# A new order for the opening of a fused attention, two-layer and soft-mixture kernel

## The chip, the cores and the metric

The kernel runs on one core of one Trainium2 chip. The number that counts is the device time of one execution in microseconds (us). A core has five engines with a queue of instructions each: PE (TensorE, the matrix engine), DVE (VectorE), ACT (ScalarE), POOL (GpSimd) and SP (SyncE, which here only issues DMAs). Each engine runs its own queue strictly in order and waits on semaphores for the others, so an instruction that waits holds up all that stands behind it on its engine.

## The reference

Three parts follow one another; all data is float32.

```python
scores = scale * np.matmul(q, k.transpose(0, 1, 3, 2))      # 4 batches, 8 heads, 576 tokens, 64 wide
scores = np.where(masks[None], scores, -1e9)                # heads 0-3: the last 32 tokens; 4-7: every 32nd token
attn = softmax(scores)
x = np.matmul(attn, v)                                      # regrouped to 2304 tokens x 512
...
h = x @ w_in                                                # 512 -> 2048
r = np.maximum(h, 0.0)
x = (r * r) @ w_out                                         # 2048 -> 512
...
logits = x @ phi                                            # 32 slots
d = softmax over tokens;  slot_input = d.T @ x
slot_out[e] = np.maximum(slot_input[e] @ w1[e], 0.0) @ w2[e]    # 8 experts, 4 slots each
out = softmax over slots @ slot_out
```

## The kernel before, in words

The 2304 tokens are handled in six blocks of 384. A block has twelve **steps** of PE work, step s = 12b + 3c + j for block b, quarter c of the 2048 hidden columns and 128 tokens j. One step is twelve matmuls of 128x128 by 128x512 (`gemm1`, line 462): four parts kc of the contraction, three matmuls each, because activations and weights are split into a rounded high part and the rest (low part). Its result goes through relu (`square`), a square (`sq`, on ACT or POOL) and a transposition on DVE (`bt_`, into the tile `gt`), and after three steps `logits` multiplies `gt` by a small matrix `pt`, which is phi folded into w_out beforehand (`matrix`: product `pp` on PE, copy to `lsb` on ACT, product `pr` on PE, transposition into `pt` on DVE). After four such `logits` the block's softmax and slot sums follow (`Dispatch`).

Attention comes in **units**: a batch and a pair of heads. Unit n of the opening is 0 to 3 for batch 0 (pairs 0 to 3) and 4 to 7 for batch 1 (pairs 2, 0, 3, 1; those of pairs 0 and 1 are first halves, part A). Pairs 0 and 1 are local, pairs 2 and 3 strided. A unit loads q, two halves of k, and v; it makes masked scores (`qa`), exponentials, a normalised copy, transposes that (for units 0 to 3 through the PSUM tile `turned`, for the others by DVE), multiplies by v (`oa`, `ob`), and writes high and low parts into the tile `xr` that the steps read. Step 0 needs the units 0 to 3.

The weights come raw, 512 KB a load (`raw0` to `raw15` for w_in, `raw16` to `raw31` for the transposed w_out), as 64-bit words that must be taken apart: `convert(m)` handles raw 2m and 2m+1 by reading the upper words (ACT, line 427), a shift (DVE, line 430) and two combinations (DVE, line 434). For w_in two casts to the high part (ACT) and two subtractions (DVE or POOL, line 443) follow.

All this is woven together in the **opening**, whose order is written out by hand: the string `HEAD` is a list of tokens, and the loop over `HEAD.split()` issues each token's instructions at that place of every queue that they use. q, v and l are loads (unit's q and k, unit's v, raw weight), w is a number of dummy matmuls, A is the next piece of a unit, C the next piece of a conversion, P the next piece of a `pt` matrix, G one kc of a step, R its relu, X its square, T its transposition, L a `logits`; f loads phi, H and Z give memory over. A letter A, D or P at the end picks the engine. Behind the opening a loop over steps puts everything else at fixed places between the steps.

Loads that are issued by SP go out in order, at most eight outstanding: each waits until the one eight places ahead has landed, and, where it overwrites a buffer, until the last reader has finished. Units 0 and 3 to 7 share one buffer for q and k, and the units from 4 on one buffer for v.

Of the kernel before, what the change touches and what calls it, by code (L numbers as in the profile page):

```python
# [17 lines left out]
NB_ATT, H, S, D = 4, 8, 576, 64  # L18
# [15 lines left out]
RAW_AT = [0, 1, 2, 20, 21, 22, 23, 0, 1, 2, 23, 0, 1, 2, 0, 1]  # L34
NY = 4
HEAD = """
l1 l0 q2 l4 q1 l8 l9 w10 A0 A2 A0 q3 v0 l3 l2 C0 A0 C0 A0 w2 A0 C0 C0 A2 C0 A0 A2 C0 w1 A1 A0 C0 C0P A0 C2 A2
A0D A1 C0P A2 A2 A0 A1 C4 A1 C4 A3 A2 A0A A1 C4 A0A A0D A2P C4 A0A A3 q4 v1 l11 l7 v2 l22 l5 l6 l16 f l18 v3
l14 A0A C4 A0A A1 A0D A0D C4 A3 w3 A0 v4 A1 C4 C1 C4D C4P A2 A0 A1 A0 A0 A3 A1P C1 A0 G0 A2A A2A C1 A2A A4 A2A
A2A C1 A2A A4 q5 l17 l10 l15 l21 A2A A2A C1 C1 A1 A4 A3 C1 C1D A4 A3 C1P A1A A1D A4 A3 A1A A2 A1A A4 A3P A1D  # L40
A2 A1D A2 A1D A2 A4 A2 A1A A2 A4P C2 A2 w4 A3 A2 C3 A2 C2 C3 A1 A3D C8 A3D C2 G0 A3A A3A A1 C2 A1 A1 A3A A3A
A1 A3A w1 G0 A3A C3 C2 A3 C3 C2 A4 C2D C2P A3 H A3 C3 A3 A3 A3 C3 A3 A3 C3 C3P A3 A4D w3 A5 A4D A4A G0 C3P C8
A5 A4A G1 A4D R0 C8 C5 G1 A5 X0P C5 C8 l23 l13 G1 C7 C8 A5 A4A G1 C5 C7 G2 A5 T0 A4A G2 R1 A5 C5 G2 X1A C5 C5
G2 A5 C5 G3 C5P A4D T1 R2 Z A4 v5 l19 l12 q6 l24 C7 G3 A4 C5P C7 G3 A4 A4 C7 G3 A4 A5P A4 C9 G4 A4 X2P C7 A5
G4 A5 C7 A5 A5 G4 C7P R3 A5 A4 G4 A5 C9 X3P A5 G5 A5 R4 A4 G5 C7D C6 X4P A5 T2 C6 G5 C11 C9 G5 C11 C6 A6 A5 C9
l25 R5 G6 C11 A6 q7 v6 l20 X5A A5 G6 C11 G6 C11 l27 G6 A6 G7 C9 R6 C6 A6 C12 P0 C6 C12 G7 A6 C12 P0 G7 A6 C6
P0 C12 C6 C6P A7 A6 X6A G7 P0 A6P A7 C12 l29 l26 l28 R7 G8 C6P A6 L0 A6 X7P C10 A6 C10 G8 A6 G8 C10 G8 T5 G9
C10 R8 G9 C10 C13 G9 A7 C13 T4 P1 X8A C13 C14 A7 T3 G9 P1 C13 A7 G10 C14 C13 A6 v7 l30 R9 A7 G10 C14 X9A G10
A6 A7 C14 l31 A6 A7P G10 A6 C14 A6 G11 R10 A6 G11 A6 X10A A6 G11 A6 A7 P1 A7 C15 A7 G11 A7 P1 P2 C15 A7 A7 L1
R11 A7 C15 P2 A7 X11P C15 P2 C15 A7 P2 A7 A7 T7 P3 T6 P3 T8 P3 L2 P3 T9 T11 T10 L3  # L50
"""
ATT_END = 48
EPS = 1e-9
# [21 lines left out]
def body(tc, qd, kd, vl, vs, win, wout, woutt, phi, w1, w2, cst, out):  # L75
    nc = tc.nc
    PE, ACT, DVE, POOL, SP = nc.tensor, nc.scalar, nc.vector, nc.gpsimd, nc.sync

    with ExitStack() as base, ExitStack() as order:
        def pool(stack, name, bufs=1, side="left", space=None, **kw):  # L80
            if space is not None:
                return stack.enter_context(tc.tile_pool(name=name, bufs=bufs, space=space, **kw))
            return stack.enter_context(tc.tile_pool(name=name, bufs=bufs, side=side, **kw))
# [16 lines left out]
        def ps(tag, name):  # L100
            if tag in ("t", "lg", "mo"):
                return late[0].tile([128, 512], F32, tag=tag, name=name, bufs={"t": 2, "lg": 1, "mo": 1}[tag])
            return pp.tile([128, 512], F32, tag=tag, name=name, bufs=2)

        c = cp.tile([128, C_END], F32, name="c")
# [25 lines left out]
        def slot(n, shape, dt, name):  # L131
# [11 lines left out]
        bufs = [  # L143
            b0,
            Buf(hp.tile([128, S + 16], F32, name="q1"), hp.tile([128, KW], F32, name="k1"),
                hp.tile([128, 8, 128], F32, name="v1"), hp.tile([128, 10, 64], F32, name="sl1"), None, None),
            Buf(hp.tile([128, S + 16], F32, name="q2"), hp.tile([128, KW], F32, name="k2"),
                hp.tile([128, 8, 128], F32, name="v2"), None, b0.ss, b0.sw),
            b0.but(v=hp.tile([128, 8, 128], F32, name="v3"), ss=hp.tile([128, 16, 18], F32, name="s3"),
                   sw=hp.tile([128, 16, 32], F32, name="sw3")),  # L150
        ]

        def load_qk(b, p, u, part="AB", queue=None):
            n = S if "B" in part else T // 2
            SP.dma_start(u.q[:, :n], qd[b, p, :, :n])
            (queue or SP).dma_start(u.k[0:64, 32:32 + n], kd[b, p, 0:64, :n])
            SP.dma_start(u.k[64:128, 32 + S:32 + S + n], kd[b, p, 64:128, :n])

        def load_v(b, p, u, part="AB"):
# [293 lines left out]
        def where(s):  # L453
            return s // 12, s % 12 // 3, s % 3

        def gemm1(s, kcs=range(4)):
            b, ch, j = where(s)
            if s not in hs:
                hs[s] = [ps("h", f"h{s}"), 0]
            for kc in kcs:  # L460
                for x, a in ((0, 0), (0, 1), (1, 0)):
                    PE.matmul(hs[s][0], xr[b % 3][:, x, kc, 128 * j:128 * j + 128], w_in[ch, kc][:, a],  # L462
                              start=hs[s][1] == 0, stop=hs[s][1] == 11)
                    hs[s][1] += 1
# [150 lines left out]
        def load_e_pair(a, b):  # L615
            load_e(lambda name: [a, b])

        def load_e_slot(n):
            load_e(lambda name: slot(n, [128, 2, 512], F32, name))

        def load_e_ring(n):
            t = ringp.tile([128, 6, 512], F32, tag=f"ring{n}", bufs=1, name=f"ring{n}_{e_next[0]}")
            for y in range(3):
                load_e(lambda name: t[:, 2 * y:2 * y + 2])

        def load_e_raw(n):
            load_e(lambda name: rawp.tile([128, 2, 512], F32, tag=f"r{n}", bufs=1, name=name))

        def load_e_x1(n):
            load_e(lambda name: x1.tile([128, 2, 512], F32, tag=f"x{n}", bufs=1, name=name))  # L630
# [26 lines left out]
        units += [Unit(b, p, b0, part, n == 0, early=n < 4) for n, (b, p, part) in enumerate(UNITS)]  # L657
        convs = [convert(m) for m in range(16)]
        mats = [matrix(h) for h in range(4)]
        gemms = {s: iter((0, 2, 1, 3)) for s in range(12)}  # L660
        load_qk(0, 0, b0, queue=ACT)
        ACT.dma_start(c, cst)
        for token in HEAD.split():
            k, e = token[0], token[-1] if token[-1] in ENG else ""
            n = int(token[1:].rstrip("ADP") or 0)
            if k == "f":
                SP.dma_start(ph, phi)
            elif k == "q":
                load_qk(units[n].b, units[n].p, units[n].u, units[n].part)
            elif k == "v":  # L670
                load_v(units[n].b, units[n].p, units[n].u, units[n].part)
# [34 lines left out]
        for n, p in zip(range(8, 4 + len(UNITS)), AT):  # L706
            un = units[n]
            at(max(48, last + 2), load_qk, un.b, un.p, un.u, un.part)
            at(max(48, last + OFF[4]), load_v, un.b, un.p, un.u, un.part)
            for k, o in zip("SCETV", OFF):  # L710
                at(p + o, un.run, k)
            last = p
        for b in range(NBLK):
            for ch in range(4):
                for j in range(3):
                    s = 12 * b + 3 * ch + j
# [52 lines left out]
        for s in range(12, NSTEP + 1):  # L769
            if s == ATT_END:  # L770
                attx.close()
                x1 = pool(base, "x1", side="right", reuse_waits="tile")
                for n in range(7):
                    load_e_x1(n)
            if s == 65:
                for n in range(3):
                    load_e_raw(n)
                load_e_pair(*(gp.tile([128, 512], F32, tag=f"g{n}", bufs=1, name=f"ge{n}") for n in (2, 3)))
            if s in (48, 60):
                load_e_ring(s // 12 - 4)  # L780
            if s == NSTEP:
                break
            for kc in range(4):
                gemm1(s, (0, 2, 1, 3)[kc:kc + 1])
                if kc == 3:
                    (last_step if s == NSTEP - 1 else square)(s)
                for fn, args in bg.get(4 * s + kc, ()):
                    fn(*args)
            if s > 60 and s % 3 == 2:
                for n in range(4 * ((s - 60) // 3), 4 * ((s - 60) // 3) + 4):  # L790
                    load_e_slot(n)
# [214 lines left out]
```

## Time and profile before

| | |
|---|---|
| median of 3 runs | 424.94 us (423.97 to 427.31) |
| the profiled execution: its own time | 426.56 us |
| its span from first to last instruction | 424.6 us |
| mean granted TensorE clock | 0.989 |
| busy share of the span: PE, DVE, ACT, POOL | 94%, 56%, 41%, 15% |
| step 0 ends | 50.65 us |
| the last `logits` of block 0 ends | 109.73 us |
| the first matmul of step 13 starts | about 114.5 us |

The profiled execution lies 1.6 us above the median and within the spread of the runs; 2 us lie outside its span. The opening is the first quarter of the span. From step 13 on PE has hardly a gap until 414 us.

### The profile page before, as it was taken

The numbers are of one execution on the slowest core, as the hardware profiler recorded it, in microseconds if no ns is written. First come the engines' busy times: TensorE is split into PE (matmuls) and PEld (weight loads), VectorE is DVE, ScalarE is ACT, GpSimd is POOL, SyncE is SP. The second block draws the span as 40 slices with busy tenths as digits, with TensorE's granted clock in tenths as the row PEclk, the third lists the DMA queues.
The fourth block names the chain that finished last, engine by engine and source line by source line (L and its number), as shares of the span: only waits on it lengthen the run. The fifth ranks groups of instructions, "written<-read, shape, count | busy, mean of one in ns | idle before, by whom it ended". The sixth has DMA issues, their size and how long they took to land.

```text
span 424.6 us, 14121 instructions
## 1 busy us (share of the span) xinstructions
PE 398.7 (94%) x6276; PEld 291.0 (69%) x6276; DVE 237.5 (56%) x511; ACT 175.8 (41%) x363; POOL 65.7 (15%) x96
## 2 busy tenths in 40 slices
PE   7877799998899999999999999999999999989993
PEld 6565586763667777677776778867887688743582
DVE  1797798977357767487667786334333422321133
ACT  1587685571133334333534455434443234211332
POOL 6222462400001110201111110000000000512000
PEclk9998999999899999999999999999999999999998
DMA  7989667741102333033252233983325495999997
GB/s 242 288 306 410 232 194 202 289 162 40 47 13 58 90 88 103 6 90 106 76 194 77 82 103 100 364 330 103 100 58 197 147 379 217 353 308 411 408 405 300
DMA packets 26844, 81.53 MB, mean 192 GB/s; under 512 B 3232, under 2 KB 4256, under 8 KB 26784
## 3 DMA queue, kind: packets, MB, share of 16 engines
q1 hardware_dynamic: 26560, 80.28, 54.2%
q8 instruction: 49, 0.80, 0.8%
q10 hardware_dynamic: 224, 0.35, 0.3%
q14 instruction: 11, 0.09, 0.1%
HBM read 75.90 MB, written 4.72 MB: 190 GB/s over the span
## 4 chain that ended last, share of the span: by engine, by line
PE 81%; DMA 8%; DVE 4%; ACT 2%; SPq 1%; issue 1%; DVEq 0%; ACTq 0%
PE h L462 46%; PE lg L508 9%; DMA k<-kd 5%; PE sa L576 4%; PE so L900 3%; PE eh L874 3%; DMA raw<-win 2%; PE ob L376 2%; PE oa L376 2%; DMA v<-vs 2%; PE qa L270 1%; PE out L918 1%; PE lr L549 1%; PE lt L560 1%; PE si L837 1%
## 5 line engine op out<-in xcount | busy, mean ns | idle before, releaser
L462 PE MATMUL h<-w,xr 128*128 128x512 f32 x864 | 219.5, 403 | 0.0
L462 PEld LDWEIGHTS h<-w,xr 128*128 128x128 f32 x864 | 158.2, 189 | 39.2 <-issue 3.2
L470 ACT ACTIVATE g<-h 128x512 f32<-128x512 f32 x71 | 42.4, 598 | 137.8 <-PE h L462 137.8
L482 DVE STREAM_TRANSPOSE gt<-g 128x512 f32<-128x512 f32 x71 | 49.9, 707 | 71.4 <-ACT g L474 59.3
L508 PE MATMUL lg<-gt,pt 32*32 32x96 f32 x3072 | 41.3, 254 | 3.4 <-DVE gt L482 2.8
L508 PEld LDWEIGHTS lg<-gt,pt 32*32 32x32 f32 x3072 | 34.4, 103 | 14.3 <-issue 5.7
L474 ACT ACTIVATE g<-g 128x512 f32<-128x512 f32 x65 | 41.0, 630 | 1.4
L349 DVE STREAM_TRANSPOSE ptl<-sl 32x320 f32<-32x320 f32 (+2 forms) x64 | 27.3, 426 | 0.8
L427 ACT ACTIVATE wo<-raw 128x512 f32<-128x512 f32 x32 | 20.8, 663 | 2.5 <-POOL w L443 1.2
L443 POOL TENSOR_TENSOR w<-y,w 128x512 fp32r<-128x512 f32 x12 | 16.2, 1358 | 36.5 <-ACT w L439 36.5
L434 DVE SCALAR_TENSOR_TENSOR wo<-raw,wo 128x512 uint32<-128x512 uint32 x32 | 21.7, 710 | 0.1
L742 POOL CAST pt<-c_all 128x192 fp32r<-128x192 f32 x2 | 0.7, 342 | 114.2 <-PE lg L508 114.2
L576 PE MATMUL sa<-g,ex 128*32 128x512 f32 x144 | 16.7, 596 | 0.0
L427 ACT ACTIVATE y<-raw 128x512 f32<-128x512 f32 x16 | 10.3, 672 | 15.4 <-DMA raw<-win 15.3
L313 POOL TENSOR_TENSOR sl<-sl,tiny 128x640 f32<-128x640 f32 (+2 forms) x9 | 10.4, 1151 | 37.9 <-DVE tiny L308 30.6
L676 PE MATMUL turned<-acc 128*128 128x128 f32 x48 | 10.1, 374 | 6.2 <-DVE pts L338 2.0
L297 POOL TENSOR_TENSOR sl<-sl,tiny 128x640 f32<-128x640 f32 (+1 forms) x6 | 7.1, 1188 | 56.6 <-DVE tiny L296 56.6
L349 DVE STREAM_TRANSPOSE pts<-sw 32x512 f32<-32x512 f32 x20 | 14.0, 702 | 0.2
L676 PEld LDWEIGHTS turned<-acc 128*128 128x128 f32 x48 | 8.6, 268 | 7.4 <-DVE pts L338 2.3
L874 PE MATMUL eh<-e,lsb 128*32 128x512 f32 x100 | 12.8, 594 | 0.4 <-ACT lsb L851 0.4
L391 ACT CAST xr<-oa 128x192 fp32r<-128x192 f32 (+2 forms) x24 | 8.5, 423 | 10.8 <-PE oa L376 10.7
L434 DVE SCALAR_TENSOR_TENSOR y<-raw,y 128x512 uint32<-128x512 uint32 x16 | 12.9, 839 | 0.2
(202 smaller groups left out, 461.6 us busy)
## 6 DMA issues: line engine op xcount, KB each, us to landing
e<-w SPq DMA_DIRECT2D x44, 512.0 KB, 7.3
raw<-win SPq DMA_DIRECT2D x16, 512.0 KB, 7.7
raw<-woutt SPq DMA_DIRECT2D x16, 512.0 KB, 5.9
raw<-wout SPq DMA_DIRECT2D x16, 512.0 KB, 4.2
ring<-w SPq DMA_DIRECT2D x15, 512.0 KB, 10.2
q<-qd SPq DMA_DIRECT2D x16, 288.0 KB, 3.9
out<-ob SPq DMA_DIRECT2D x12, 384.0 KB, 5.0
k<-kd SPq DMA_DIRECT2D x31, 144.0 KB, 4.5
```

The lines of the kernel that those rows point to most:

```text
L349: yield "T", lambda e, d=dst, s_=src: DVE.transpose(out=d, in_=s_)
L376: PE.matmul(o[bank][64 * h:64 * h + 64, col:col + w1_ - w0], u.v[0:k, t, 64 * h:64 * h + 64], rhs, start=start, stop=stop, skip_group_chec ...
L427: ACT.activation(y[0][:, z], raws[2 * m + z][:, :, 1].bitcast(F32), AF.Prelu, scale=2.0 ** -112, alpha=2.0 ** 32)
L434: DVE.scalar_tensor_tensor(out=yb, in0=raws[2 * m + z][:, :, 0], scalar=29, in1=yb, op0=ALU.logical_shift_right, op1=ALU.bitwise_or)
L462: PE.matmul(hs[s][0], xr[b % 3][:, x, kc, 128 * j:128 * j + 128], w_in[ch, kc][:, a], start=hs[s][1] == 0, stop=hs[s][1] == 11)
L470: ACT.activation(gs[s], h, AF.Relu)
L474: ACT.activation(gs[s], gs[s], AF.Square)
L482: DVE.transpose(out=gts[b, ch][:, j], in_=gs[s])
L508: PE.matmul(lgs[b][q(y), a, 0:T // 4], pt[q(a), 512 * ch + f:512 * ch + f + 32], g[q(a), :, f:f + 32], start=ch == 0 and n == 0, stop=ch = ...
L576: PE.matmul(o[32 * ch:32 * ch + 32, :], ex_[:, 32 * j:32 * j + 32], gs[12 * self.b + 3 * ch + j], start=j == 0, stop=j == 2, skip_group_ch ...
L676: PE.matmul(warm, dummy, dummy, start=True, stop=True)
L874: PE.matmul(hps[g][n][q(j), :], siT[:, kc, :], cols(ex[0, g, j, kc], 512 * n, 512), start=kc == 0, stop=kc == 3, skip_group_check=True)
```

## The change

The two new places where the constants `c` and two halves of keys are loaded, the condition that keeps these halves from being loaded twice, and the first step of block one (step 12), whose four parts and relu are now tokens of the opening (`G12`, `R12`), so that the loop leaves them out:

```diff
@@ load_qk
-            (queue or SP).dma_start(u.k[0:64, 32:32 + n], kd[b, p, 0:64, :n])
+            if b or p not in (1, 2):
+                (queue or SP).dma_start(u.k[0:64, 32:32 + n], kd[b, p, 0:64, :n])
@@ before the loop over HEAD
-        gemms = {s: iter((0, 2, 1, 3)) for s in range(12)}
+        gemms = {s: iter((0, 2, 1, 3)) for s in range(13)}
+        SP.dma_start(c, cst)
         load_qk(0, 0, b0, queue=ACT)
-        ACT.dma_start(c, cst)
+        for p in (2, 1):
+            ACT.dma_start(bufs[p].k[0:64, 32:32 + S], kd[0, p, 0:64])
@@ the loop over steps
-                gemm1(s, (0, 2, 1, 3)[kc:kc + 1])
-                if kc == 3:
+                if s > 12:
+                    gemm1(s, (0, 2, 1, 3)[kc:kc + 1])
+                if kc == 3 and s > 12:
                     (last_step if s == NSTEP - 1 else square)(s)
@@ HEAD, the first and the last line (all fourteen differ)
-l1 l0 q2 l4 q1 l8 l9 w10 A0 A2 A0 q3 v0 l3 l2 C0 A0 C0 A0 w2 A0 C0 C0 A2 C0 A0 A2 C0 w1 A1 A0 C0 C0P A0 C2 A2
+q2 l1 l4 l0 l5 q1 v2 w6 A2 A0 A0 q3 l9 v0 l15 l18 A0 A2 A0 A2 A0 A2 A0 C2 A0 A2 C0 A0 w3 A1 A2 C0 A0D A3 C2 A2
...
-R11 A7 C15 P2 A7 X11P C15 P2 C15 A7 P2 A7 A7 T7 P3 T6 P3 T8 P3 L2 P3 T9 T11 T10 L3
+C15 A6 L2 A6 C15 A6 A6 A6 A6 A6 A6 C15 A7 T9 P3 A7 A7 P3 T11 G12 T10 P3 G12 P3 R12 L3
```

`HEAD` holds the same pieces of work in another order, with five squares fewer on POOL (they stand on ACT), and with 9 dummy matmuls in place of 24. Line numbers above 157 are one higher in the new kernel, those above 665 three higher.

On SP, in the opening's loads up to the last that step 0 needs, these rows stood before (`vl` and `vs` are the v of local and strided pairs, `raw` a raw weight, `q0`, `k0` the shared buffer):

```order
L155 DMA q0_93<-qd 128x576
L156 DMA k0_94<-kd 64x576
L157 DMA k0_94<-kd 64x576
L162 DMA v1_104<-vl 128x640
L410 DMA raw11_349<-win 128x1024
L410 DMA raw7_351<-win 128x1024
L164 DMA v2_108<-vs 128x1024
L410 DMA raw22_354<-woutt 128x1024
L410 DMA raw5_356<-win 128x1024
L410 DMA raw6_358<-win 128x1024
L410 DMA raw16_360<-woutt 128x1024
```

Now, from the same load of unit 4's q on:

```order
L155 DMA q0_93<-qd 128x576
L157 DMA k0_94<-kd 64x576
L158 DMA k0_94<-kd 64x576
L411 DMA raw8_345<-win 128x1024
L163 DMA v1_104<-vl 128x640
L411 DMA raw6_348<-win 128x1024
L670 DMA ph_90<-phi 128x128
L411 DMA raw3_351<-win 128x1024
L411 DMA raw11_353<-win 128x1024
L411 DMA raw2_355<-win 128x1024
L411 DMA raw16_357<-woutt 128x1024
L165 DMA v3_109<-vs 128x1024
```

Unit 2's v now stands far ahead of this piece, raw 2 and 3 (for step 0) have moved behind it, raw 5 and 15 and 18 ahead of it, and unit 3's v (`v3`, before two rows behind the piece shown) ends the list with one raw weight less in front of it.

On PE, at the end of the opening, before (`pp`, `pr` with the number of the matrix; `lg0` the `logits` of block 0; `h12`, `h13` steps; `qa1_0` the scores of unit 8):

```order
L524 MATMUL pr2_1278<-lsb_81,c_78 128x512
L376 MATMUL oa1_1_1281<-ptl_91,v0_95 64x160 x2
L376 MATMUL oa1_1_1281<-ptl_91,v0_95 64x64 x2
L517 MATMUL pp3_1291<-wo14_1107,ph_90 32x512 x2
L517 MATMUL pp3_1291<-wo15_1190,ph_90 32x512 x2
L524 MATMUL pr3_1299<-lsb_81,c_78 128x512
L508 MATMUL lg0_997<-gt0_2_1289,pt_79 32x96 x64
L508 MATMUL lg0_997<-gt0_3_1366,pt_79 32x96 x64
L462 MATMUL h12_1434<-w0_246,xr1_88 128x512 x3
L462 MATMUL h12_1434<-w1_254,xr1_88 128x512 x3
```

The same place now:

```order
L463 MATMUL h12_1235<-w1_417,xr1_88 128x512 x3
L377 MATMUL oa1_3_1246<-pts_92,v0_95 64x72 x8
L377 MATMUL ob1_3_1247<-pts_92,v0_95 64x72 x8
L509 MATMUL lg0_916<-gt0_2_1233,pt_79 32x96 x64
L377 MATMUL oa1_1_1342<-ptl_91,v0_95 64x160 x2
L377 MATMUL oa1_1_1342<-ptl_91,v0_95 64x64 x2
L518 MATMUL pp3_1349<-wo14_1078,ph_90 32x512 x2
L518 MATMUL pp3_1349<-wo15_1243,ph_90 32x512 x2
L463 MATMUL h12_1235<-w2_588,xr1_88 128x512 x3
L525 MATMUL pr3_1362<-lsb_81,c_78 128x512
L463 MATMUL h12_1235<-w3_591,xr1_88 128x512 x3
L509 MATMUL lg0_916<-gt0_3_1347,pt_79 32x96 x64
```

Step 12 stands between the last pieces of the opening, `logits` 2 has moved ahead of matrix 3, and the values of unit 6 (`oa1_3`, `ob1_3`) and unit 7 (`oa1_1`) have moved to the end; before, those of unit 6 stood in step 10.

## Rows read from the trace of the kernel before

**Rows 1.** The page, chain that ended last: shares of the span by engine.

```profile
PE 81%; DMA 8%; DVE 4%; ACT 2%; SPq 1%; issue 1%; DVEq 0%; ACTq 0%
```

**Rows 2.** Busy time by stretch: the first 42 us, two inside, two near 108 us.

```profile
core 0: us, PE busy (x) PEld busy (x) DVE busy (x) ACT busy (x) POOL busy (x), PEclk, DMA share, GB/s
0.00:42.00 42.00, 31.91 (x456) 24.88 (x457) 27.46 (x61) 23.43 (x53) 15.42 (x28) 0.96 0.93 311
24.00:28.00 4.00, 3.11 (x37) 2.72 (x38) 3.92 (x8) 3.35 (x8) 1.38 (x2) 1.00 0.77 219
28.00:36.00 8.00, 5.73 (x119) 4.43 (x116) 7.48 (x16) 6.67 (x20) 3.09 (x3) 1.00 1.03 403
...
104.00:108.00 4.00, 1.47 (x112) 1.00 (x94) 1.92 (x4) 0.00 (x0) 0.00 (x0) 1.00 0.02 4
108.00:112.00 4.00, 4.00 (x124) 3.27 (x102) 0.00 (x0) 0.00 (x0) 0.00 (x0) 0.57 0.02 4
```

**Rows 3.** Timeline of the first 11 us: start, us, engine, line, work [idle before].

```profile
1.51 0.60 ACTq L662 DMA_DIRECT2D c<-cst  x1
...
7.51 1.14 PE L227 MATMUL wide<-c 128*128 128x128 f32 x4 [1.56 <-DMA c<-cst]
...
10.43 0.69 DVE L241 TENSOR_REDUCE tiny<-wide 128x8 f32<-128x512 f32 x1 [8.05 <-PE wide L237]
```

**Rows 4.** The chain of waits, first 35 us: start, us, what (two of its loads).

```profile
1.17 4.87 DMA k<-kd
...
26.81 7.29 DMA v<-vs
```

**Rows 5.** Timeline from unit 3's v to the end of step 0.

```profile
32.87 0.33 SPq L164 DMA_DIRECT2D v<-vs  x1
...
44.33 0.72 PE L376 MATMUL oa<-pts,v 128*64 128x72 f32 x16
...
45.48 1.06 PE L327 MATMUL turned<-c,sw 128*64 128x128 f32 x8
...
47.62 0.69 DVE L392 TENSOR_TENSOR xr<-ob,xr 128x192 fp32r<-128x192 f32 x2
...
48.57 0.94 PE L676 MATMUL turned<-acc 128*128 128x128 f32 x6 [2.03 <-DVE pts L338]
...
49.71 0.94 PE L462 MATMUL h<-w,xr 128*128 128x512 f32 x3
```

**Rows 6.** Timeline, 65 to 116 us: unit 5's values, and the opening's end.

```profile
65.44 0.75 PE L376 MATMUL oa<-ptl,v 128*64 128x160 f32 x8
...
95.67 1.06 PE L517 MATMUL pp<-wo,ph 128*32 128x512 f32 x8
...
96.80 0.58 ACT L520 COPY lsb<-pp 128x512 f32<-128x512 f32 x1 [0.43 <-PE pp L517]
...
102.14 1.13 PE L524 MATMUL pr<-lsb,c 128*128 128x512 f32 x2 [0.76 <-ACT lsb L520]
...
103.30 0.72 DVE L527 STREAM_TRANSPOSE pt<-pr 128x512 f32<-128x512 f32 x1 [0.65 <-PE pr L524]
...
107.66 2.07 PE L508 MATMUL lg<-gt,pt 32*32 32x96 f32 x128 [2.06 <-DVE gt L482]
109.66 3.34 PE L462 MATMUL h<-w,xr 128*128 128x512 f32 x9
...
113.73 2.34 PE L462 MATMUL h<-w,xr 128*128 128x512 f32 x9
```

**Rows 7.** Tile raw, 80 to 100 us: ns min/median/max; issue to landing.

```profile
L427 ACT ACTIVATE wo<-raw x8: 655/660/697, 79.9 to 94.8; 128x512 f32<-128x512 f32 x8
L434 DVE SCALAR_TENSOR_TENSOR wo<-raw,wo x8: 649/682/1095, 82.8 to 98.9; 128x512 uint32<-128x512 uint32 x8
...
DMA to landing us min/median/max: 3.8/4.7/5.5
```

**Rows 8.** Timeline of SP: the two issues of raw21 and raw23.

```profile
43.48 10.63 SPq L410 DMA_DIRECT2D raw<-woutt  x2
```

More of the change, by code (lines that the diff above doesn't have):

```diff
@@ L36 @@
 HEAD = """
-l1 l0 q2 l4 q1 l8 l9 w10 A0 A2 A0 q3 v0 l3 l2 C0 A0 C0 A0 w2 A0 C0 C0 A2 C0 A0 A2 C0 w1 A1 A0 C0 C0P A0 C2 A2
[L38 to L46, printed above, removed]
@@ L47 @@
-P0 C12 C6 C6P A7 A6 X6A G7 P0 A6P A7 C12 l29 l26 l28 R7 G8 C6P A6 L0 A6 X7P C10 A6 C10 G8 A6 G8 C10 G8 T5 G9
-C10 R8 G9 C10 C13 G9 A7 C13 T4 P1 X8A C13 C14 A7 T3 G9 P1 C13 A7 G10 C14 C13 A6 v7 l30 R9 A7 G10 C14 X9A G10
-A6 A7 C14 l31 A6 A7P G10 A6 C14 A6 G11 R10 A6 G11 A6 X10A A6 G11 A6 A7 P1 A7 C15 A7 G11 A7 P1 P2 C15 A7 A7 L1
-R11 A7 C15 P2 A7 X11P C15 P2 C15 A7 P2 A7 A7 T7 P3 T6 P3 T8 P3 L2 P3 T9 T11 T10 L3
+q2 l1 l4 l0 l5 q1 v2 w6 A2 A0 A0 q3 l9 v0 l15 l18 A0 A2 A0 A2 A0 A2 A0 C2 A0 A2 C0 A0 w3 A1 A2 C0 A0D A3 C2 A2
@@ new lines @@
+A0 C2 C0 A1 A0A C2 A0A A0A C2 C2 A1 A2P C2 A1 A0A C2D A1 A0A C0 A0A A0A A3 q4 l8 v1 l6 f l3 l11 l2 l16 v3 C0
+A0A A1 C2P A2 A3 C0 A1 A0 A2A A2A A1 A2A A2A A1P A2A A3 A2A A2D A0 A2D A0 A0 A1 A3 C0 C0P A0 A3 A2 A1A A3 A1A
+C0P G0 A1D A2 A1D A2 A2 A1D A2 A1D C4 A2 A2 A1A A2 A1A A2 C4 A3D A1 C3 C4 C4 A3 A1 C4 A1 C4 G0 A1 C4 A1 C4P
+A3D A4 A3A A3D C1 A3D A4 q5 l17 l10 l7 C4P A3D C1 A3D A4 A3A A3A C1 A4 C8 C1 A4 A3 C1 C1 A4 C1 C1D H A3 A4 A3
+G0 A3 C1P A3 A3 A3 C8 A3 A4P A3 A5 C8 C5 G0 C8 l23 l22 l14 l19 l21 l12 C5 G1 C8 R0 G1 C5 C3 G1 X0A C5 G1 C5 G2
@@ new lines @@
+C5 C3 R1 G2 C5 C5D G2 X1A C3 G2 C3 G3 C3 T1 C5P R2 G3 C3 T0 A5 q6 X2A C3P A4 A5 C9 T2 C9 A5 C3D G3 A4A C9 A5
+G3 C7 A5 G4 C7 A4D A5 G4 A4A C9 l25 l13 l24 v4 A4A C6 G4 C7 A4A G4 A4A C9 A4A A6 R3 C7 P0 R4 C7 A6 C7 A4D A5P
+G5 P0 A6 Z C7 C7P A5 G5 A5 X3A A5 A6 A5 A5 C6 C7P G5 A5 A5 A6 G5 A5 X4A A6 P0 C6 C11 G6 C11 P0 G6 C12 A6 G6
+C12 C11 G6 R5 C6 A4 v5 R6 C11 l26 l20 X5A C11 L0 A4 C12 A4 A4 C6 C6 G7 C12 l28 l27 C6 G7 C12 l29 q7 A4 G7 C6D
+G7 A4 A6P G8 A4 R7 C6P A4 G8 A6 X7A G8 A6 X6P C10 G8 A6 C10 G9 A6 R8 G9 C10 X8A G9 A4 C10 G9 C10 G10 C13 T3
@@ L51 @@
+G10 C13 T4 C14 A7 G10 C14 C13 G10 R9 T5 P1 C14 X9A A7 R10 C13 G11 P1 A7 G11 X10A C13 A7 C14 l31 G11 A7 C14 G11
+A7 P1 A7 R11 A5 v6 l30 A7P P1 X11A P2 A7 A5 A7 A7 L1 A5 P2 A7 A7 A7 A7 P2 A7 T6 G12 P2 G12 C15 T8 A6 v7 C15 T7
+C15 A6 L2 A6 C15 A6 A6 A6 A6 A6 A6 C15 A7 T9 P3 A7 A7 P3 T11 G12 T10 P3 G12 P3 R12 L3
 """
```

## The prediction

> **What bounds the kernel now.** I read the chain that ended last first: PE holds 81% of it and loads 8% [rows 1]. Behind 114 us PE works without a gap worth naming, so nothing there can be gained or lost by an opening that leaves the later order alone; what counts is how much earlier PE gets to step 13. In the chain of waits the first 35 us are loads [rows 4]. The stretches say why: DMA engines are busy 0.93 of the first 42 us and move 311 GB/s, and from 28 to 36 us they are full at 403 GB/s [rows 2]. From 50 to 95 us PE is dense with steps 0 to 11, and the end, from 95.67 to 109.73, has gaps: PE waits for transpositions that wait for `logits` 2, which wait for matrix 3 [rows 6]; in 104 to 108 PE is busy 1.47 of 4 us, and then the granted clock is 0.57 for four microseconds [rows 2], the lower of the two levels (1.2 GHz) for most of that stretch.
>
> So the opening has three sections: up to the end of step 0 (50.65, the end of its last matmuls [rows 5]), from there to the start of `pp2` (95.67 [rows 6]), and the rest to step 13. I cost the change by section.
>
> **The constants and the split keys.** The masks start at 7.51, having waited 1.56 for c, which was issued at 1.51 behind unit 0's loads; the first scores reach DVE at 10.43 [rows 3]. The last half of unit 0's keys had landed at 6.04 (1.17 + 4.87 [rows 4]). With c first the masks no longer wait; the products now end the wait. Two more key halves run beside them: 0.49 MB with c in all, 1.6 us at 311 GB/s, of which a part comes in front. Products then start at about 7 and not at 9.3, and DVE 2 to 2.5 us sooner. I count nothing of that by itself, because what is late next is the queue of loads, which this does not shorten; the full 2 us go into the low end of the range.
>
> Two queues in place of one could also raise the rate of the first 24 us. The rows show 403 GB/s at share 1.03 while one queue alone was feeding [rows 2], so the engines and not the queue were the limit there. The Trainium skill, page "DMA: Bandwidth & Descriptors", section "Issuing engines are not separate DMA queues", says that loads from several engines run on the same sixteen DMA engines, and that starting them from several saves only the time of starting; by it the split is worth nothing beyond the issue, and the trace agrees as far as these stretches go. Were it otherwise, the first 24 us at 403 would bring all loads some 3 us forward; that is a rival below.
>
> **Step 0.** It needs raw 0 to 3, and the units 0 to 3, the last of whose loads is v3. Sizes follow from the shapes (512 KB a raw or a strided v, 576 KB q and k, 320 KB a local v). Before, 14 raws stand up to v3, 12.27 MB in all; now 13, 11.74 MB. 42 us at 311 are 13.06 MB, so 12.27 had moved at about 40.0; 0.53 MB less is 1.3 us at 403: 38.7. Before, the queue also ran dry while SP waited to reuse unit 3's buffer: in 24 to 28 us the share is 0.77 against 1.03 [rows 2], a loss of 1.0 us. Now four loads (raw9, v0, raw15, raw18) stand in front of that wait, as cover: 37.7. Without the cover it is 38.7 again. Unit 3's values started at 44.33, 4.3 after the data had moved; 512 KB take 1.3 us to move and at the least 3.8 from issue to landing [rows 7], so 2.5 is the floor of that lag. The values start between 40.2 and 42.0; I take 40.6, nearer the floor, since the transposed scores that made the rest of the lag come earlier now. From there to the end of step 0 it was 6.3 us, with 2.0 of PE waiting for copies out of `turned` for unit 4 [rows 5]; that transposition now stands behind step 0. 4.3 to 6.3; I take 4.4. **Step 0 ends at 45.0** (44.5 to 48.3) in place of 50.65. Raw 2 is two loads ahead of v3, its conversion (ACT, DVE, ACT, POOL) runs beside the values and ends with them.
>
> **Steps 1 to 11.** Before, 45.0 us from the end of step 0 to `pp2`. In the new order the stretch to unit 5's values loses those (0.75) and unit 6's (two halves like the one of 0.72, which overlap: 1.2), and gains unit 4's transposes (1.06): 44.1. The gaps in it are assumed alike: DVE's list to the end of the opening has 170 instructions in place of 168, and ACT has five more, the squares from POOL. Unit 5's values start at 45.0 + 44.1 = 89.1.
>
> **The end of the opening.** Here the change adds a wait. The v of unit 6 may be issued only when unit 5's values are done, since they share a buffer, and raw30 stands behind it on SP. Matrix 3 waits for raw30. So: values 0.75, two issues and the wait 0.8 (90.7), landing 4.7 (3.8 to 5.5 [rows 7]; 95.4), upper words of raw30 and raw31 2 x 0.66 (96.7), shift and first combination about 2 x 0.68 (98.1), unit 6's low parts in between 2 x 0.7 (99.5), second combination 0.68 (100.2), `pp3` 1.06, copy 0.58, `pr3` 1.13, transposition 0.72 (103.7), the last `logits` at full clock 1.7 (105.4), and 0.6 for eight hand-overs: **106.0**, against 109.73. PE meanwhile has the work that stands there (`pp2`, two `logits`, `pr2`, unit 6's and 7's values, step 12), some 11 of the 17 us, so step 12 runs in what would be gaps. Before, it came after the last `logits`: its nine first matmuls took 3.34, most of it at the lower clock, where the later nine took 2.34 [rows 6]; with unit 8's scores and its last three, step 13 began at 114.5, 4.8 us after that `logits`. Now only the scores lie between (0.8): 106.8.
>
> **Sum.** 114.5 - 106.8 = 7.7 us: 3.7 from an earlier `logits`, 4.0 from step 12. Behind it nothing moves against PE: the softmax of block 0 follows `logits` 3 at a distance of 2.2 us of PE work in place of 6.3, and needs one copy on ACT (0.5). The profiled execution had 426.56 us, so 418.9; it lies 1.6 above the median, so **417.3**.
>
> **The rivals.**
> *The loads bind as before.* If the rate of the first 28 us stays and the start of values keeps its lag of 4.3, step 0 ends near 49.3, the rest follows 4.3 later: a gain of 3.4, 421.5. For it: the same bytes, the same engines. Against: a raw less and the covered gap. 0.17.
> *The two queues carry more.* Loads 3 us earlier, step 0 at 42: 414.3. Against it stand the full rows of 28 to 36 us, and the page named above. 0.08.
> *The end's loads take long.* Unit 2's v took 7.29 from issue to landing [rows 4], with a full queue; if v6 and raw30 did so, matrix 3 is 2.6 later: 419.9. Against: nearly nothing else is loading then (share 0.02 in 104 to 108). 0.10.
> *Slower: SP stands at raw23.* Its buffer is raw16's, so SP waits for a conversion on DVE; it stood for 10 us at that load before too [rows 8], but now raw22, 14, 19, 21, 12 and unit 6's q stand behind it, and ACT reads raw19, 14 and 12 before the relu of step 3. If raw23 goes out 1.5 us after step 0, raw12 lands 4.7 + 5 x 1.3 later, 12.7 after step 0, and ACT's relu is due at 15. From about 4 us after step 0 each microsecond of delay is one of PE's; at 12 the gain is gone, at 16 the kernel is slower by 1%, 429.5. DVE has the conversion right behind unit 3's low parts, which speaks against. 0.05.
>
> **How the numbers follow.** The forecast gets 0.60. A measurement of this kernel tells 1% from no change, since the runs span 424 to 427. Faster by over 1% (under 420.7): forecast, two queues, most of the third rival, and the lower part of the first: 0.78. Within 1%: 0.17. Slower: 0.05. The range: with step 0 at 48.3 and slow landings at the end (0.8) the gain is 3.6, and 2.6 with a gap more in the steps: 422.5; with the 2 us of the start passed on in full and the quickest landings it is 10.6, and a microsecond of scatter: 413.4.
>
> **What would show it.** c landing before 5 us and the first reduction on DVE near 8. Unit 3's values on PE at 40 to 42, and the end of step 0 near 45; if the values start early and step 0 ends late, the copies of `turned` or the conversion of raw 2 and 3 are the cause. ACT or DVE idle before the last conversion, released by raw30, and `pp3` near 100. No stretch of the lower clock at step 12, and unit 8's scores right after the last `logits` near 106. The prediction is wrong if steps 1 to 11 take over 47 us, which would be ACT with its five squares, or if PE waits behind step 13.

## The result and the profile after

| | before | after |
|---|---|---|
| median | 425.44 us (423.68 to 428.85, 20 runs) | 422.11 us (419.86 to 426.36, 20 runs) |
| the profiled execution: time, span | 426.56, 424.6 us | 423.04, 421.2 us |
| mean granted clock in it | 0.989 | 0.986 |

The ratio is 0.9914 (0.989 to 0.9937): a gain of 0.9%, 3.7 us by the ratio and 3.3 by the medians, where 7.6 was forecast. The time lies in the stated range, close to its upper end (424.9 less 2.6 is 422.3; the prediction wrote 422.5). Ratios, here and in the table below, leave out runs over 1.5% above a kernel's fastest, which are one of the 20 here and four of the ten of e2, whose median of all is 429.85 us against 426.76.

First the opening. These rows are from timelines of the changed kernel, in the places of [rows 3], [rows 5] and [rows 6]; columns as there.

```profile
8.08 0.69 DVE L242 TENSOR_REDUCE tiny<-wide 128x8 f32<-128x512 f32 x1 [5.70 <-PE wide L238]
...
39.55 0.72 PE L377 MATMUL oa<-pts,v 128*64 128x72 f32 x16
...
46.61 0.59 ACT L471 ACTIVATE g<-h 128x512 f32<-128x512 f32 x1
...
88.88 0.75 PE L377 MATMUL oa<-ptl,v 128*64 128x160 f32 x8
...
95.34 1.30 ACT L428 ACTIVATE wo<-raw 128x512 f32<-128x512 f32 x2 [3.86 <-DMA raw<-woutt]
...
98.80 0.75 PE L377 MATMUL oa<-ptl,v 128*64 128x160 f32 x8 [0.99 <-PE lg L509]
99.48 1.52 PE L518 MATMUL pp<-wo,ph 128*32 128x512 f32 x8
100.93 0.97 PE L463 MATMUL h<-w,xr 128*128 128x512 f32 x3
101.74 1.12 PE L525 MATMUL pr<-lsb,c 128*128 128x512 f32 x2
102.30 1.26 PE L463 MATMUL h<-w,xr 128*128 128x512 f32 x3
103.67 1.69 PE L509 MATMUL lg<-gt,pt 32*32 32x96 f32 x128
105.30 0.74 PE L271 MATMUL qa<-k,q 128*32 128x128 f32 x18
...
106.09 1.65 PE L463 MATMUL h<-w,xr 128*128 128x512 f32 x6
```

The first reduction on DVE starts at 8.08 (before 10.43), unit 3's values at 39.55 (44.33), the relu of step 0 at 46.61 (51.24; the matmuls of step 0 end at 46.0 by the trace, before at 50.65), unit 5's values at 88.88 (65.44 in the old order), the upper words of raw30 at 95.34, `pp3` at 99.48, and the last `logits` ends at 105.4 (109.73). Two pieces of step 12 stand among these as filling. Step 13 starts at 106.09; before, its first matmul came three matmuls of 0.26 us into the row of 113.73, at 114.5. So the opening is 8.4 us shorter in this execution; the forecast was 7.7.

Only 3.4 us of it are left at the end of the span. The next fence is the view of PE's waits from 114 us on, of the changed kernel: line, what it waited for, us in total, times, longest.

```profile
PE h L463 <- issue: 2.2, 2, 1.5
PE lg L509 <- issue: 1.2, 1, 1.2
...
PE sa L577 <- issue: 0.4, 1, 0.4
...
PE so L904 <- issue: 0.3, 1, 0.3
```

The same view of the kernel before has none of these four lines; it has the same waits for `acc`, `gt` and `lsb` (0.8, 0.8 and 0.4 us), which the changed kernel has too (0.9, 0.8 and 0.4). So PE stops five times, 4.1 us in all, for nothing that the program makes it wait for. A timeline of PE around three of the stops:

```profile
202.04 0.93 PE L509 MATMUL lg<-gt,pt 32*32 32x96 f32 x60
204.15 0.98 PE L509 MATMUL lg<-gt,pt 32*32 32x96 f32 x68 [1.18 <-issue]
...
270.37 0.81 PE L550 MATMUL lr<-lsb,c 128*128 128x384 f32 x2
272.66 2.33 PE L463 MATMUL h<-w,xr 128*128 128x512 f32 x9 [1.48 <-issue]
...
329.94 1.68 PE L509 MATMUL lg<-gt,pt 32*32 32x96 f32 x128 [0.39 <-DVE gt L483]
331.55 0.98 PE L463 MATMUL h<-w,xr 128*128 128x512 f32 x3
333.21 5.07 PE L463 MATMUL h<-w,xr 128*128 128x512 f32 x21 [0.69 <-issue]
```

The first stop is in the middle of a `logits`, which has no wait inside; the two others stand a few matmuls behind one (the one at 271.2 eight, the one at 332.5 three). Now the instructions between one stop and the next, from the busy time by stretch (the counts in brackets are matmuls and weight loads; the stretches run from the last matmul before a stop to the last before the next):

```profile
core 0: us, PE busy (x) PEld busy (x) DVE busy (x) ACT busy (x) POOL busy (x), PEclk, DMA share, GB/s
202.98:271.17 68.19, 66.84 (x1148) 50.79 (x1147) 43.92 (x91) 29.42 (x59) 5.60 (x6) 1.00 0.47 160
271.17:332.53 61.36, 59.10 (x896) 44.27 (x895) 23.03 (x50) 24.01 (x45) 0.00 (x0) 1.00 0.43 149
332.53:365.61 33.08, 32.32 (x512) 26.00 (x512) 8.86 (x18) 10.77 (x21) 4.87 (x18) 1.00 0.78 282
365.61:412.10 46.49, 44.56 (x636) 24.82 (x637) 10.17 (x30) 10.61 (x31) 4.87 (x14) 1.00 0.99 378
```

Matmuls and weight loads together are 2295, 1791, 1024 and 1273: 9, 7, 4 and 5 times 256, less 9, 1, 0 and 7. (PE's semaphore instructions, which this view leaves out, are 9, 2, 0 and 7 in the trace.) The stops lie a whole number of 256 instructions apart, to within one in this count. And the page has a queue that I had read past, the same in both kernels:

```profile
q8 instruction: 49, 0.80, 0.8%
```

That is 49 packets of 0.80 MB, 16 KB each, and PE's 6246 matmuls and 6246 weight loads are 48.8 times 256. PE's code thus comes in pieces of 256 instructions, by DMA, while it runs. The view of DMA has one such packet shortly ahead of the end of a stop: one from 201.6 to 202.9, none from 199 to 201.6; it had moved by 202.79, and PE went on at 204.15. The Trainium skill, page "Runtime: NRT & Kernel Launch", section "Instruction fetch mechanics", says that code is refilled in blocks of 16 KiB, 256 instructions, by a DMA queue of the engine's own, and that crossing a block's end is mostly hidden. The trace agrees with the size and not with the hiding: 4.1 us here.

That gave **theory A**: where these pieces begin decides. A piece with a whole `logits` in it (256 instructions in 1.69 us, the row of 103.67) is used up before PE can go on with the next. The change moves the beginnings, since it has 62 PE instructions fewer ahead of step 13: 15 dummy matmuls of four instructions each, and two semaphore instructions. **Rival B**: the stops come from what the new opening leaves behind, other buffers or loads at other moments.

### The profile page after: what moved, and what is told of

Read it like the earlier page. It is cut to its first block, busy times and chain, and to the rows that moved or that the text cites. A ratio compares the mean times of both kernels' runs of the same rounds, so it can differ in the third digit from the quotient of the medians.

```text
span 421.2 us, 14061 instructions
## 1 busy us (share of the span) xinstructions
PE 397.7 (94%) x6246; PEld 289.2 (69%) x6246; DVE 233.2 (55%) x513; ACT 177.8 (42%) x368; POOL 60.6 (14%) x89
## 4 chain that ended last, share of the span: by engine, by line
PE 87%; DVE 4%; DMA 3%; issue 3%; ACT 2%; SPq 0%; DVEq 0%; ACTq 0%
PE h L463 48%; PE lg L509 9%; PE sa L577 4%; PE so L904 4%; PE eh L878 3%; PE ob L377 2%; PE oa L377 2%; DMA raw<-win 2%; PE qa L271 1%; DMA k<-kd 1%; PE pp L518 1%; PE out L922 1%; PE lr L550 1%; PE turned L328 1%; PE pr L525 1%
## 5 line engine op out<-in xcount | busy, mean ns | idle before, releaser
L475 ACT ACTIVATE g<-g 128x512 f32<-128x512 f32 x70 | 44.1, 630 | 1.4
L444 POOL TENSOR_TENSOR w<-y,w 128x512 fp32r<-128x512 f32 x11 | 17.1, 1565 | 27.9 <-ACT w L440 27.8
L435 DVE SCALAR_TENSOR_TENSOR wo<-raw,wo 128x512 uint32<-128x512 uint32 x32 | 20.8, 683 | 0.1
L581 DVE SCALAR_TENSOR_TENSOR acc<-acc,st,sa 128x512 f32<-128x512 f32 x6 | 4.5, 748 | 13.6 <-PE sa L577 13.6
L393 DVE TENSOR_TENSOR xr<-oa,xr 128x192 fp32r<-128x192 f32 (+2 forms) x24 | 9.4, 421 | 4.3 <-ACT xr L392 4.2
L431 DVE TENSOR_SCALAR wo<-wo 128x1024 uint32<-128x1024 uint32 x16 | 10.7, 668 | 1.7 <-ACT wo L428 1.2
L393 DVE TENSOR_TENSOR xr<-ob,xr 128x192 fp32r<-128x192 f32 (+2 forms) x24 | 9.5, 426 | 3.7 <-ACT xr L392 3.7
```

The source lines that it names most:

```text
L393: low.append(lambda e, d=d, src=src: DVE.tensor_tensor(out=d[1], in0=src(), in1=d[0].bitcast(F32), op=ALU.subtract))
L435: DVE.scalar_tensor_tensor(out=yb, in0=raws[2 * m + z][:, :, 0], scalar=29, in1=yb, op0=ALU.logical_shift_right, op1=ALU.bitwise_or)
L444: ENG[e].tensor_tensor(out=w[:, 1], in0=y[0][:, z], in1=w[:, 0].bitcast(F32), op=ALU.subtract)
L475: ACT.activation(gs[s], gs[s], AF.Square)
```

## The experiments

Step 13's start and the time from there to the end of the span are read from each profiled execution. "Stops" adds up PE's waits for issue behind step 13, without three of 0.2 us that every kernel has at line 290 or 291. Ratios are to the kernel before on the same chip.

| kernel | step 13 starts | to the end | stops | ratio |
|---|---|---|---|---|
| before | 114.5 | 310.1 | 0 | 1 |
| after | 106.1 | 315.1 | 4.1 | 0.9914 (0.989 to 0.9937) |
| e1: 15 one-column dummies | 113.9 | 310.4 | 0 | 0.9978 (0.9945 to 1.0011) |
| e2: before, 15 dummies fewer | 112.7 | 313.7 | 3.5 | 1.0018 (0.9973 to 1.0063) |
| e3: step 12 in the loop | 109.5 | 315.6 | 4.7 | 0.9997 (0.9961 to 1.0032) |
| e5: one load later | 103.2 | 316.0 | 4.5 | 0.9884 (0.9838 to 0.993) |
| e6: 15 small dummies at 8 us | 111.0 | 310.5 | 0.4 | 0.9878 (0.985 to 0.9906) |
| e7: e6, first loads as before | 110.2 | 309.5 | 0 | 0.9912 (0.9887 to 0.9937) |
| e8: 32 small dummies | 107.9 | 316.7 | 5.5 | 0.9942 (0.9911 to 0.9973) |
| e9: dummies in gaps | 109.1 | 309.8 | 0 | 0.9865 (0.9837 to 0.9893) |
| e10: 15 small dummies at step 13 | 102.7 | 310.4 | 0 | 0.9746 (0.9697 to 0.9794) |
| e11: e10, dummies moved | 105.5 | 311.1 | 0 | 0.9761 (0.9717 to 0.9805) |

Theory A has a check that takes in all twelve traces. PE's matmuls, weight loads and semaphore instructions can be counted from the first one on; then 35 of PE's waits for issue last 0.25 us or more, before and behind step 13. Of these, 33 stand behind an instruction whose number is 192 or 193 more than a multiple of 256, and in each of the 33 PE goes on 1.2 to 1.6 us after the end of a code packet. (The other two, 1.05 us in the opening of e3 and 0.34 us in that of e9, do neither.) In four of the five stops of the changed kernel the packet had ended before PE stopped, at 332.53 by 0.8 us; what the 1.2 to 1.6 us are needed for the traces don't show.

### e1 and e2: the pieces moved, both ways

In e1 15 dummies of one column bring the changed kernel's steps to the pieces of the kernel before (`y15` behind the first `G0`); in e2 the kernel before loses 15 dummies.

```diff
+            elif k == "y":
+                for _ in range(n):
+                    PE.matmul(warm[:, 0:1], dummy, dummy[:, 0:1], start=True, stop=True)
-C0P G0 A1D A2 A1D ...
+C0P G0 y15 A1D A2 A1D ...
```

```diff
-l9 w10 A0 ... A0 w2 A0 ... C0 w1 A1 ... A2 w4 A3 ... A3A w1 G0 ... A4D w3 A5
+l9 w6 A0 ... A0 A0 ... C0 A1 ... A2 A3 ... A3A G0 ... A4D A5
```

> The changed kernel with 15 more dummy matmuls of one column each, put where PE waits from 28.4 to 30.6 us anyway; with them, PE's instructions from step 13 on have the numbers that they have in the kernel before (to within two). In the changed kernel the opening ends 8.4 us earlier, but PE stops without a wait in the program at 202.98 (1.2 us), 271.18 (1.5), 332.53 (0.7), 365.61 (0.4) and 412.10 (0.3), each time a multiple of 256 PE instructions apart. Theory A: PE's code comes in pieces of 256 instructions by DMA, and PE stops where a piece comes late; where the pieces begin decides that. Then the five stops vanish or shrink to what the kernel before has (none over 0.3 without a named wait): from the first matmul of step 13 to the end of the span 310 to 311 us in place of 315.1, and a time of 418 (ratio 0.982 to 0.986). Rival B: the stops come from what the new opening leaves (other buffers, loads at other moments); then they stay where they are, 315 from step 13 to the end, 422.

> The kernel before with 9 dummy matmuls in place of 24, as in the changed kernel; nothing else of the change. PE's instructions from step 13 on then have the numbers of the changed kernel (to within three). Theory A (code in pieces of 256): stops of 0.3 to 1.5 us appear in the steps, near 210, 279 and 340 us, which are the same places in the program as in the changed kernel; from step 13 to the end 314 to 315 in place of 310.1, and a time near 429 (ratio 1.01). Rival B (the rest of the new opening): no stops, 310 from step 13 to the end; a time of 425, or up to 2 us more by a lower clock in the first 50 us, where the dummies are missing.

In e1 the view of PE's waits behind 112 us has no stop, and in e2 stops are there, at the places in the program where the changed kernel has them: in the `logits` of 208 us, in the step behind that of 334 and in the work of the last block; those of 271 and 412 us have no counterpart. From e2's view:

```profile
PE h L462 <- issue: 1.6, 1, 1.6
PE hold L798 <- issue: 1.1, 1, 1.1
...
PE lg L508 <- issue: 0.8, 1, 0.8
```

From step 13 to the end e1 takes 310.4 and e2 313.7 us. So the new opening is not needed for stops, and with it they can be gone: B falls, for both parts of it. Both times missed what I expected. In e2's execution the opening was 1.8 us shorter, which hides half of the stops; whether the missing dummies made it so is not shown. In e1 the dummies were not cheap, and the end of the opening got stops of its own:

```profile
29.00 4.56 PE L682 MATMUL turned<-acc 128*128 128x1 f32 x30
...
33.66 1.97 DVE L339 COPY ptl<-turned 32x320 f32<-32x320 f32 x4 [5.01 <-PE turned L682]
...
100.52 0.35 PE L377 MATMUL ob<-pts,v 128*64 128x72 f32 x4 [0.47 <-issue]
...
105.34 0.35 PE L509 MATMUL lg<-gt,pt 32*32 32x96 f32 x4 [2.89 <-issue]
```

The dummies took 4.56 us, in part at the lower clock, and DVE's copies out of the same tile waited 5.01 us for them. Step 13 came 7.8 us later than in the changed kernel, which is nearly all of what the opening had gained. Up to 3.4 us of these are the two stops, which the changed kernel does not have: they come from the shift of the pieces and not from what the dummies cost.

### e3: step 12 back in the loop

```diff
-        ... G12 P2 G12 C15 ... T11 G12 T10 P3 G12 P3 R12 L3
+        ... P2 C15 ... T11 T10 P3 P3 L3
-                if s > 12:
+                if True:
...
```

> The changed kernel with step 12 taken out of the opening and back in the loop; the number of PE instructions ahead of step 13 is the same. By the prediction's own sum step 12 in the gaps of the opening was worth 4.0 us: last logits near 105 to 106 as now, step 13 4.0 later (110), time 426. Rival: the gaps are filled by PE work that only shifts, and then step 12 is worth 2 us or less: 424 or less. The stops in the steps stay in size under theory A (the pieces lie as in the changed kernel).

The difference of the ratios, 0.9997 less 0.9914, is 0.8% or 3.5 us, and the intervals leave some 1.8 us to either side. In the profiled execution the last `logits` ends at 105.5, as in the changed kernel (105.4), and step 13 starts 3.9 us behind that end in place of 0.7: 3.2 us. The term of 4.0 us was right within this. Four of the five stops are where they were; the one of 0.3 us at 412 is gone.

### e5: does a piece need a load in its way?

```diff
-            at(max(48, last + OFF[4]), load_v, ...)
+            at(max(48, last + OFF[4]) + 4 * (last == 110), load_v, ...)
```

> The changed kernel with one load of values, the one issued at 199.05 us, put four places (one step, some 3 us) later in the loop; its data is needed at 212. Nothing of PE's code moves. The piece of code that PE waits for at 202.98 starts to move at 201.68, when that load is nearly done (it landed at 201.93). Theory A1: the piece was late because it stood behind the load; then the stop of 1.2 us at 203 vanishes, the others stay, 421 in place of 422. Theory A2: a piece takes as long without a load, and only the short time in which 256 instructions with a whole logits run counts; then the stop at 203 stays at 1.0 to 1.3 us.

The stop in that `logits` is 0.7 us by the waits view, where the changed kernel has 1.2 and e3, with the load in place, 1.6. It did not vanish, as A1 had it, and it is under the 1.0 to 1.3 us of A2; the stop in the work of the last block (line 577), 0.4 us in the changed kernel, is 1.3 us here. So the load is not needed for a stop; how much of the difference is due to it can't be told from three executions. The stop at 332.5 of the changed kernel speaks for the same: in the view of DMA from 330.5 to 331.9 the code packet is the only one that moved. There the piece that begins at 329.95, with a `logits`, was used up at 332.53, and PE went on at 333.21: 3.3 us from one piece to the next on idle DMA engines. That is an estimate for one place, from these rows.

### e6 to e9: cheaper dummies, other places

A matmul of 32x32 by one column costs little (15 of them some 0.5 us in e10), and `warm` is not read by anyone at 8 us:

```diff
+            elif k == "y":
+                for x in range(n):
+                    y = slice(32 * (x % 4), 32 * (x % 4) + 32)
+                    PE.matmul(warm[y, 0:1], dummy[0:32, 0:32], dummy[0:32, 0:1], ...)
-... l15 l18 A0 A2 A0 ...
+... l15 l18 A0 y15 A2 A0 ...
```

e7 is e6 with the first loads of the kernel before; e8 has `y32`; e9 has `y6`, and nine full dummies into `wide` in two gaps.

> The changed kernel with 15 dummy matmuls of 32x32 by one column (60 PE instructions) where PE waits from 8.2 to 9.3 us for keys; nothing waits for what they write. It moves the pieces of code as the one-column dummies did, which took 4.56 us and held up the copies of turned, but at a cost under 1 us that lies in a gap. Theory A (stops where a piece of 256 instructions comes late): no stop in the steps, 304 us from step 13 to the last matmul in place of 309.7; step 13 at 103 to 106 as in the changed kernel; a time of 416.5 to 417.5 (ratio 0.977 to 0.982). Rival: the gain that the pieces give back is lost again in the opening, as in the first try: 420 or more.

> The kernel with 15 small dummies, with the constants and the keys loaded as before the change: c on ACT's queue behind unit 0's keys, all key halves by SP or ACT as they were. The prediction counted the earlier start (DVE 2 to 2.5 us sooner) as nothing, since the loads bind up to step 0: then step 0 ends at most 1 us later and the time is 417 to 418. Rival: the earlier start is passed on in full, step 13 is 2 us or more later, time 419 or more.

> The changed kernel with 32 small dummies (128 PE instructions, half a piece of code) in the same gap. The opening as with 15 small ones, at most 0.7 us later. Theory A: the stops of the changed kernel at 203, 271 and 333 us are not there, since no piece begins where it did; whether others come is open, and any that come stand multiples of 256 PE instructions from each other; step 13 to the last matmul between 304 and 310 us. Rival B (stops belong to places in the program): the three stops are there as before, 309 to 310.

> The changed kernel with the same shift of 60 PE instructions, but made of 6 small dummies at 8.2 us and of 9 full ones (128x128) in the gaps of PE at 28.4 (six) and 42.6 us (three), into a buffer that nothing else uses then. No stop in the steps. If what PE does in these gaps decides the drops of the granted clock (0.5 from 31 to 36 and from 44.3 to 47.7 us in the changed kernel), the mean granted clock is 0.993 or more and the time 415 to 416; if not, 417 as with the small ones, or up to 1 us more for the dummies themselves.

e6 cleared the steps and got only a third of what I expected, since the shift also moved the pieces of the opening's end. A timeline of PE there:

```profile
98.12 0.35 PE L377 MATMUL ob<-pts,v 128*64 128x72 f32 x4 [0.68 <-issue]
98.39 1.73 PE L509 MATMUL lg<-gt,pt 32*32 32x96 f32 x124
102.39 0.35 PE L509 MATMUL lg<-gt,pt 32*32 32x96 f32 x4 [2.27 <-issue]
```

Four matmuls before the end of `logits` 2 PE stops for 2.27 us, and `pp3`, which stands behind it in PE's order, starts at 103.46 and not at 99.48. e7 and e9 have the same stop (2.21 and 2.89 us), as e1 had. In e8 the stops of 271 and 333 us are gone, and four others have come, in `logits` that had none in the changed kernel, the longest of 2.01 us; one of 1.48 us came to the end of the opening. All lie multiples of 256 instructions from each other, to within one. The stop of 203 us is still in the same `logits`, against my expectation, but not at the same matmul. Its rows in e8, and ahead of them those of the longest:

```profile
147.36 1.57 PE L509 MATMUL lg<-gt,pt 32*32 32x96 f32 x115
150.95 0.39 PE L509 MATMUL lg<-gt,pt 32*32 32x96 f32 x13 [2.01 <-issue]
...
207.39 1.66 PE L509 MATMUL lg<-gt,pt 32*32 32x96 f32 x124
209.67 0.35 PE L509 MATMUL lg<-gt,pt 32*32 32x96 f32 x4 [0.62 <-issue]
```

In the changed kernel PE stopped there behind 60 of the 128 matmuls, here behind 124: 64 matmuls with their weight loads are 128 instructions, the half piece by which the code was moved. So a stop belongs to no place in the program: it comes where a piece ends in or just behind a fast stretch.

e7 against e6 prices the constants and the split keys. Its first reduction on DVE is at 11.85 us against 8.38, 3.5 later, but step 0 ends only 0.6 us later (47.7 against 47.1), and step 13 starts at 110.2 against 111.0. The times are 0.9912 and 0.9878 of the kernel before, with intervals that overlap: by these 1.4 of the 3.5 us arrive, and the noise leaves room for none and for most of them.

e9's granted clock stayed at 1.00 up to 98 us; e6 had 0.50 from 32 to 36. By the times they are the same (0.9865, 0.9878).

### e10 and e11: the pieces of the old steps, the pieces of the new opening

```diff
+        hs[13] = [ps("h", "h13"), 0]
+        for x in range(15):
+            PE.matmul(hs[13][0][q(x % 4), 0:1], dummy[0:32, 0:32], dummy[0:32, 0:1], ...)
         bg = {}
```

The dummies stand behind the last `logits` of the opening and write into the accumulator of step 13, which overwrites them. In e11, besides, `w6` is gone from the start, and four and two dummies stand in the gaps.

> The changed kernel with the 15 small dummies (60 PE instructions, 0.7 us) behind the last logits of the opening, ahead of step 13: the opening keeps the pieces of code of the changed kernel (no stop of over 0.3 us at its end), the steps get those of the kernel before. The first try with small dummies cleared the steps (304.8 us from step 13 on) but brought two stops of 0.7 and 2.3 us to the end of the opening, each a piece of code that came late, and step 13 at 110.95. Theory A: step 13's own work at 104 to 107, 304 us from there to the last matmul, no stop over 0.4 us in either part: last matmul at 408 to 411, time 415.5 to 418.5, ratio 0.979 to 0.983. That is also the prediction's 417.3, which had left the stops out. Rival: what the pieces give back in the steps is taken somewhere else again; 420 or more.

> The same, and the six dummies that run from 1.3 to 4.2 us moved into PE's gaps at 28.4 (four) and 42.6 us (two), so that the opening's pieces of code begin where they did. With dummies in these gaps the granted clock stayed at 1.0 up to 98 us in the earlier run. If that holds, the drops to 0.5 between 28 and 48 us go, and the time is 0.5 to 1.5 us below that of the kernel with the small dummies alone; if the dummies at the start matter for the clock, a drop comes earlier and the time is the same or up to 1 us more.

e10 takes 415.67 us (414.93 to 417.08), 2.5% less than the kernel before. From its timeline, and the stretches of its granted clock (the column before the last two) beside those of the changed kernel:

```profile
101.51 0.42 PE L705 MATMUL h<-acc 32*32 32x1 f32 x24
...
102.72 1.68 PE L463 MATMUL h<-w,xr 128*128 128x512 f32 x6
```

```profile
28.00:36.00 8.00, 4.76 (x101) 3.56 (x101) 7.49 (x19) 5.99 (x12) 2.52 (x2) 1.00 1.01 393
36.00:48.00 12.00, 9.12 (x67) 7.15 (x68) 11.79 (x23) 9.63 (x22) 2.75 (x3) 1.00 0.70 250
```

```profile
28.00:32.00 4.00, 1.64 (x12) 1.23 (x12) 3.93 (x10) 3.23 (x8) 0.00 (x0) 0.80 1.03 402
32.00:36.00 4.00, 4.00 (x28) 3.07 (x25) 2.54 (x6) 1.91 (x5) 1.33 (x2) 0.50 1.03 406
...
44.00:48.00 4.00, 4.00 (x14) 3.25 (x14) 3.30 (x7) 2.56 (x6) 0.00 (x0) 0.57 0.71 224
```

No stop is left, in the steps or in the opening. The opening of e10 is that of the changed kernel in its instructions up to the dummies, and yet 3.4 us shorter. One difference is the clock: the changed kernel's profiled execution had the lower clock (0.50 is 1.2 GHz) from 32 to 36 and for most of 44 to 48, where the first steps run, and e10's had not. e5, with the same opening and no drop in these stretches, had step 13 at 103.2. So the 8.1 us between the two profiled spans (421.2 and 413.1) are not all due to the pieces; from step 13 on it is 4.7. Executions at the same mean granted clock, 0.994 or 0.995, span 419.1 to 420.1 us in the changed kernel and 413.1 to 413.8 in e10, some 6 us apart, so that about one microsecond stays unexplained. e11 is the same as e10 within its interval, and its execution had a drop before 28 us instead (0.50 from 20 to 24, 0.77 from 24 to 28), as the second of its expectations has it. What sets these drops off I could not settle: kernels with the same opening have them in one execution and not in another, and filling the gaps, tried in e9 and e11, changed no time that can be measured.

## Why the prediction was wrong, step by step

- **The constants and the keys** were counted as nothing. DVE starts near 8 as foreseen (8.08), and e7 puts at 1.4 us what arrives of 3.5, within a noise as large. Not refuted, and not priced more closely.
- **Step 0.** Unit 3's values at 40.6 (40.2 to 42.0): 39.55, a little earlier than its range. Step 0's end at 45.0 (44.5 to 48.3): 46.0, with its last matmuls at the lower clock; in e10, without that, 43.1. In the range, 1.0 late. The cover of four loads held: the DMA share from 24 to 28 us is 0.96, where it was 0.77.
- **Steps 1 to 11.** Unit 5's values at 89.1: 88.88. That it fits so well is luck: the stretch from step 0's end was forecast at 44.1 us and took 42.9 (42.1 in e10), and this made up for step 0, which ended late in an execution with the lower clock there.
- **The end of the opening.** The chain over raw30 came as written: upper words after 95.4 (95.34), `pp3` at 100.2 (99.48), the last `logits` to its end at 106.0 (105.4), step 13 at 106.8 (106.1). ACT waited 3.86 us for raw30, as the added wait says. Step 12 was worth 4.0; e3 says 3.2 to 3.5. No lower clock at step 12.
- **The step that failed** is the sentence "Behind it nothing moves against PE", and with it the first paragraph's "nothing there can be gained or lost by an opening that leaves the later order alone". The later order was the same; the numbers of its instructions were not. Measured, from step 13 to the end of the span: 315.1 in place of 310.1, 5.0 us lost, of which 4.1 are the stops themselves; the rest, about 0.2 a stop, may be the overlap of matmuls that each stop breaks, which was not tried. 8.4 less 5.0 is the 3.4 of the span. With the pieces put right (e10) the loss is 0.3, and the kernel is faster than the forecast (415.67 against 417.3). So the gain of the opening was of about the forecast size, and the cost behind it, put at nothing, was 5.0 us.

None of the rivals had this mechanism: the text's last sentence, "if PE waits behind step 13", named only the symptom. The trace of before had the sign, in the fast part that I had read for other waits, in `logits` 2, with no semaphore behind it:

```profile
105.19 0.41 PE L508 MATMUL lg<-gt,pt 32*32 32x96 f32 x19 [0.47 <-issue]
```

## What to carry to other kernels

Where PE ran 256 short instructions in 1.7 us, its own code was a stream that came late, and an edit that adds or takes away instructions ahead of such a stretch moves all the places where that can happen. So look in the view of waits for "issue" without a semaphore, count the instructions between two such stops, and if the count is a multiple of 256, shift the stream with a few instructions that cost little, behind the part that must not move; try a few shifts, since one that clears one part can hurt another (e6). And compare two kernels stretch by stretch before crediting an edit: here the opening was 8.4 us shorter and the span 3.4.

## What the runs showed of the hardware

- PE's code came in packets of 16 KB (49, 0.80 MB), and of PE's 35 waits of 0.25 us or more without a semaphore, in twelve kernels, 33 lay multiples of 256 instructions from the others of their trace (to within one), and ended 1.2 to 1.6 us after a code packet. They took 0.3 to 2.9 us each, 0.7 us in one place where nothing else moved on the DMA engines.
- In this fully unrolled program the place of the pieces made up to 6.3 us, 2%, of the time from step 13 on (e8 and e10: 316.7 and 310.4 us for the same work).
- 15 matmuls of 32x32 by one column, 60 instructions, took some 0.5 us (101.39 to 101.93 in e10); 15 of 128x128 by one column took 4.56 (e1), in part at the lower clock.
